# Half of one head's store issued by GpSimd instead of SyncE, in four transfers of 7, 34, 6 and 17 partitions

## The chip, the cores and the metric

The kernel runs on one core of a Trainium2 chip. A core has five engines with an instruction queue each: PE (TensorE, matrix multiplication), DVE (VectorE), ACT (ScalarE), POOL (GpSimd) and SP (SyncE, which computes nothing and issues transfers). Transfers between main memory (HBM) and the on-chip memory (SBUF) are carried by the core's 16 DMA engines. The metric is the device time of one execution in microseconds (us); smaller is better.

## The reference

Linear attention with the feature map elu(x) + 1, for one batch, 32 heads, a sequence of 2048 and a head width of 128, in bfloat16:

```python
phi_q = jnp.where(q > 0, q + 1, jnp.exp(q)) + 1e-6
phi_k = jnp.where(k > 0, k + 1, jnp.exp(k)) + 1e-6
kv = jnp.einsum("bhsd,bhse->bhde", phi_k, v)
z = jnp.einsum("bhsd->bhd", phi_k)
num = jnp.einsum("bhqd,bhde->bhqe", phi_q, kv)
den = jnp.einsum("bhqd,bhd->bhq", phi_q, z)[..., None] + 1e-6
return num / den
```

For each head three arrays of 512 KB are read and one of 512 KB is written: 48 MB in and 16 MB out in all.

## The kernel before

One head is one tile: the 2048 rows of a head lie on 128 partitions, 16 rows (NT) of 128 numbers on each, so a partition holds 4096 contiguous bytes of an input or of the output. The 32 heads run one after the other, and the stages of neighbouring heads overlap.

The steps of a head h, by the names that the program gives them:

- ldk, ldq, ldv: the loads, issued by SP (L367), each into one of 7 buffers.
- ek, em: exp of k on ACT (L384), min with 1 plus 1e-6 on DVE (L387). rkp: max of k with 0 on POOL (L394). Since elu(x) + 1 is min(exp x, 1) + max(x, 0), phi_k is the sum of the two, and it is never formed: PE multiplies each of them by v and adds up in PSUM.
- v1: POOL copies v beside a column of ones (L398), so that kv and z come out of one product. kv: 32 products on PE (L405). kvs: the result goes to SBUF as bfloat16 (L410, DVE).
- T, eq, emq, rqa, rqb: q is transposed on PE (L417) and mapped in the same way on ACT and DVE (L421, L423, L427, L430).
- n: the products with kv and z on PE (L441, L446, L448), into PSUM. r: the reciprocal of the denominator (L464, with L461 ahead of it for the part i = 1). f: DVE multiplies and writes the head's output tile in SBUF (L468). This runs in two parts, f{h}.0 for 12 of the 16 rows of a partition and f{h}.1 for the last 4; the last head has three parts.
- st: SP issues the store (L477), from one of 12 output buffers, as soon as the f steps that it reads are done.

The order on each engine is written out by hand in ORDER (L105 to L166); an engine runs its list from front to back, and each entry waits for semaphores only where its inputs or its buffer need it. Semaphores are counted per engine, and per buffer for transfers. At the end of POOL's list stand v130.0, rkp31.0 and v131.0 (L152). At the end of SP's list, after the last load (ldq31.0), stand the stores st18.0 to st30.0 and the three parts of head 31's (L163, L164).

Three heads are stored in more than one transfer. FEW (L64) gives for heads 4, 8 and 17 a list of (first partition, end partition, n), one transfer each; st_rows and st_parts (L67, L71) read it, and some (L347) issues it. With n = 16 it is an ordinary transfer of those partitions. With another n the program builds the transfer itself, with n as the outermost dimension of both sides (L356), for SP's queue. A partition range of 96 to 128 with n = 4 is a transfer of four times 8 partitions.

After all work SP waits for the semaphore of each output buffer, the last head's last (L492 to L494), and the program ends.

Of the kernel before, what the change touches and what calls it, by code (L numbers as in the profile page):

```python
# [11 lines left out]
NI, NO, NE, NR, NV, NQ, NK = 7, 12, 2, 2, 2, 2, 2  # L12
# [41 lines left out]
def na(h):  # L54
    return NA[h]


def groups(h):
    if h == NH - 1:
        return ((0, 2, 3, 0), (6, 2, 3, 2), (12, 2, 2, 4))  # L60
    return ((0, 4, 3, 0), (12, 2, 2, 4))


FEW = {4: ((0, 96, 16), (96, 120, 3), (120, 128, 4)), 8: ((0, 96, 16), (96, 128, 4)), 17: ((0, 96, 16), (96, 128, 4))}  # L64


def st_rows(h, i):  # L67
    return FEW[h][i] if h in FEW else (0, P, 16)


def st_parts(h):  # L71
    if h in FEW:
        return WHOLE * len(FEW[h])
    return ((0, 6), (6, 12), (12, 16)) if h == NH - 1 else WHOLE
# [22 lines left out]
def rqb_parts(h):  # L97
    if na(h) == 16:
        return ()
    if h == NH - 1:  # L100
# [48 lines left out]
        v16.0 rkp7.0 v17.0 rkp8.0 v18.0 rkp9.0 v19.0 rkp10.0 v110.0 rkp11.0 v111.0 rkp12.0 v112.0 rkp13.0 v113.0  # L149
        rkp14.0 v114.0 rkp15.0 v115.0 rkp16.0 v116.0 rkp17.0 v117.0 rkp18.0 v118.0 rkp19.0 v119.0 rkp20.0 v120.0  # L150
        rkp21.0 v121.0 rkp22.0 v122.0 rkp23.0 v123.0 rkp24.0 v124.0 rkp25.0 v125.0 rkp26.0 v126.0 v127.0 rkp27.0
        rkp28.0 v128.0 v129.0 rkp29.0 rkp30.0 v130.0 rkp31.0 v131.0  # L152
    """,
    "SP": """
        ldk0.0 ldk1.0 ldq0.0 ldv1.0 ldk2.0 ldq1.0 ldv2.0 ldk3.0 ldq2.0 ldv3.0 ldk4.0 ldq3.0 ldv4.0 ldq4.0 ldk5.0
# [22 lines left out]
class Program:  # L178
# [10 lines left out]
    def add(self, eng, key, fn, deps=(), dma=None, inc=True):  # L189
        assert key not in self.op, key  # L190
        self.op[key] = (eng, fn, tuple(deps), dma, inc)
# [71 lines left out]
def bass_standalone__linear_attn_elu__prompt_kernel(nc: bass.Bass, q: bass.AP, k: bass.AP, v: bass.AP, out: bass.AP):  # L263
# [11 lines left out]
    with ExitStack() as es:  # L275
# [25 lines left out]
        pr = Program(sem)  # L301
        add = pr.add
# [44 lines left out]
        def some(e, of, to, p0, p1, n):  # L347
            of = of.rearrange("p j d -> p (j d)")[p0:p1]
            to = to.rearrange("(p j) d -> p (j d)", j=NT)[p0:p1]
            if n == 16:  # L350
                return e.dma_start(to, of)
            to = to.rearrange("(n p) e -> n p e", n=n)
            side = lambda ap, dims: mybir.PhysicalAccessPattern(
                ap=[list(d) for d in dims], offset=ap.offset, dtype=ap.tensor.dtype, memref=ap.tensor.name,
                memsetref=ap.tensor.name + "_set", bass_ap=ap)
            return e.add_instruction(mybir.InstDMACopy(  # L356
                name=nc.get_next_instruction_name(), engine=e.engine,
                ins=[side(of, [of.ap[0], [NT * D, 1], of.ap[1]])], outs=[side(to, to.ap)],
                queue="qSPDynamicHW", mode="Copy"))
# [15 lines left out]
        def head(h):  # L375
# [49 lines left out]
            n = na(h)  # L425
# [47 lines left out]
                                [[m, nb], [1, m], [0, D]]), op=ALU.mult)  # L473
                add("DVE", f"f{h}.{i}", g, [f"r{h}.{i}"] + freed(NO, h, ("st", st_parts)))
            for i, (a, b) in enumerate(st_parts(h)):
                add("SP", f"st{h}.{i}", lambda e, a=a, b=b, i=i: some(
                    e, o_sb[:, h % NO], of[h], *st_rows(h, i)) if h in FEW else e.dma_start(rows(of, h)[:, a:b], o_sb[:, h % NO, a:b]),  # L477
                    [f"f{h}.{j}" for j, (t0, nb, m, b0) in enumerate(groups(h)) if t0 < b and a < t0 + nb * m],
                    dma=f"o{h % NO}")

        for h in range(NH):
            head(h)
# [7 lines left out]
        for e, engine in (("POOL", nc.gpsimd), ("SP", nc.sync), ("ACT", nc.scalar), ("PE", nc.tensor), ("DVE", nc.vector)):  # L490
            pr.emit(e, engine)
        last = f"o{(NH - 1) % NO}"  # L492
        for name in [f"o{s}" for s in range(NO) if f"o{s}" in pr.count and f"o{s}" != last] + [last]:
            nc.sync.wait_ge(pr.get(name), pr.count[name])  # L494


# [26 lines left out]
```

## Time and profile before

| what | value |
|---|---|
| time, median of 3 runs | 168.81 us (168.54 to 169.3) |
| the profiled execution, its own time | 168.74 us |
| its span, first to last instruction | 167.4 us |
| granted TensorE clock, mean | 0.997 |
| HBM read, written | 50.33 MB, 16.78 MB |
| mean DMA rate | 403 GB/s |
| packets on SP's queue (q1), ACT's (q10) | 9663, 144 |
| a store of 512 KB, issue to landing | 19.1 us median, 3.3 to 20.6 |
| last load (ldq31) issued | 129.79 us |
| last copy of GpSimd (v131.0) | 148.68 to 150.17 us |

The profile is taken from one execution; times in it count from the first instruction. The busy time of PE is modelled and doesn't mean that it runs at its peak. The span leaves out 1.34 us of the execution's own time. Six waits of SP at L494 stand at the very end of the span, the first at 166.1 and the last at 167.4.

There is no queue of GpSimd's in the trace: it issues no transfer in this kernel. Besides SP's and ACT's queues there are two that fetch instructions (q8 and q14, 27 packets).

### The profile page before, as it was taken

What the parts mean: (1) busy time and instruction counts of PE and PEld (TensorE: products, weight loads), DVE (VectorE), ACT (ScalarE), POOL (GpSimd) and SP (SyncE); (2) the same over time, 40 slices, a digit from 0 to 9 for tenths busy, and PEclk for the clock granted to TensorE, in tenths of its full rate; (3) what the DMA queues carried; (4) which work ended last, traced back from release to release, by engine and by line L of the source; (5) the groups of instructions that cost most, each with busy time, mean ns of one, the idle gap of its engine ahead of it and who ended that gap; (6) DMA issues with size and microseconds to landing.
All of it is one profiled execution on the core that took longest, in us unless ns stands there. A gap on an engine that the chain in (4) does not pass through costs nothing.

```text
span 167.4 us, 6190 instructions
## 1 busy us (share of the span) xinstructions
PE 156.7 (94%) x2716; PEld 151.2 (90%) x2716; DVE 154.4 (92%) x300; ACT 149.5 (89%) x102; POOL 94.1 (56%) x71
## 2 busy tenths in 40 slices
PE   6999969999999999999999999999999999999740
PEld 2579859999999999999999999999999999999640
DVE  0389999999999999999999999999999999999990
ACT  4899949999999999999999999999999999995700
POOL 2779646656656666655555566666555555670000
PEclk9999999999999999999999999999999999999998
DMA  5999999999999999999999999999999999999995
GB/s 206 432 423 419 395 423 388 419 409 415 411 419 407 407 427 411 417 395 421 415 389 425 418 414 420 426 407 423 402 442 390 425 416 428 405 409 415 414 376 226
DMA packets 9834, 67.51 MB, mean 403 GB/s; under 512 B 2095, under 2 KB 2479, under 8 KB 6831
## 3 DMA queue, kind: packets, MB, share of 16 engines
q1 hardware_dynamic: 9663, 66.59, 97.3%
q8 instruction: 21, 0.34, 0.8%
q10 hardware_dynamic: 144, 0.52, 0.8%
q14 instruction: 6, 0.05, 0.1%
HBM read 50.33 MB, written 16.78 MB: 401 GB/s over the span
## 4 chain that ended last, share of the span: by engine, by line
PE 88%; DVE 8%; issue 0%; POOL 0%; POOLq 0%
PE la L405 34%; PE la L446 17%; PE la L417 17%; PE la L448 16%; PE la L339 5%; DVE la L468 4%; DVE la L387 1%; DVE la L423 1%; DVE la L464 1%; DVE la L430 0%; PE la L441 0%; DVE la L461 0%; DVE la L410 0%; POOL la L324 0%; POOL la L323 0%
## 5 line engine op out<-in xcount | busy, mean ns | idle before, releaser
L394 POOL TENSOR_SCALAR la<-la 128x2048 bf16<-128x2048 bf16 (+1 forms) x32 | 60.5, 1892 | 49.9 <-PE la L405 46.6
L468 DVE TENSOR_TENSOR la<-la 128x1536 bf16<-128x1536 f32 (+2 forms) x65 | 77.7, 1196 | 0.2
L446 PE MATMUL la<-la 128*128 128x129 bf16 x512 | 67.0, 219 | 0.1
L448 PE MATMUL la<-la 128*128 128x129 bf16 x512 | 67.0, 219 | 0.0
L421 ACT ACTIVATE la<-la 128x2048 bf16<-128x2048 bf16 (+2 forms) x35 | 60.2, 1730 | 5.3 <-PE la L448 4.0
L384 ACT ACTIVATE la<-la 128x2048 bf16<-128x2048 bf16 (+1 forms) x33 | 61.3, 1860 | 2.5 <-DMA la<-in_k_dram 2.5
L405 PE MATMUL la<-la 128*128 128x129 bf16 x1024 | 63.4, 220 | 0.0
L405 PEld LDWEIGHTS la<-la 128*128 128x128 bf16 x1024 | 59.5, 98 | 0.4
L448 PEld LDWEIGHTS la<-la 128*128 128x128 bf16 x512 | 49.5, 97 | 0.0
L446 PEld LDWEIGHTS la<-la 128*128 128x128 bf16 x512 | 47.9, 97 | 0.3 <-DVE la L410 0.3
L398 POOL COPY la<-la 128x1024 int32<-128x1024 int32 (+1 forms) x33 | 34.4, 1042 | 5.4 <-PE la L405 3.4
L417 PE MATMUL la<-la 128*128 128x128 bf16 x512 | 34.0, 219 | 1.6 <-DVE la L430 1.6
L427 ACT ACTIVATE la<-la 128x1024 bf16<-128x1024 bf16 (+1 forms) x32 | 33.5, 1047 | 0.0
L417 PEld LDWEIGHTS la<-la 128*128 128x128 bf16 x512 | 30.0, 98 | 2.4 <-DVE la L430 1.8
L387 DVE TENSOR_SCALAR la<-la 128x2048 bf16<-128x2048 bf16 (+1 forms) x33 | 24.8, 751 | 6.1 <-ACT la L384 6.1
L423 DVE TENSOR_SCALAR la<-la 128x2048 bf16<-128x2048 bf16 (+2 forms) x35 | 25.1, 717 | 0.3 <-ACT la L421 0.3
L441 PE MATMUL la<-la 128*128 128x3 bf16 (+1 forms) x128 | 21.6, 169 | 1.8 <-DVE la L468 1.4
L430 DVE TENSOR_SCALAR la<-la 128x1024 bf16<-128x1024 bf16 x31 | 20.5, 661 | 0.0
L441 PEld LDWEIGHTS la<-la 128*128 128x128 bf16 x128 | 12.5, 97 | 2.1 <-DVE la L468 1.5
L464 DVE RECIPROCAL la<-la 128x12 f32<-128x12 f32 (+2 forms) x65 | 12.9, 200 | 1.3 <-PE la L448 0.3
L339 PE MATMUL la<-la 128*128 128x480 bf16 x28 | 8.8, 464 | 1.5 <-POOL la L324 1.5
L410 DVE CAST la<-la 128x129 bf16<-128x129 f32 x32 | 7.8, 244 | 0.1
(16 smaller groups left out, 11.9 us busy)
## 6 DMA issues: line engine op xcount, KB each, us to landing
la<-in_k_dram SPq DMA_DIRECT2D x32, 512.0 KB, 19.2
la<-in_q_dram SPq DMA_DIRECT2D x32, 512.0 KB, 19.6
la<-in_v_dram SPq DMA_DIRECT2D x31, 512.0 KB, 19.4
out_dram<-la SPq DMA_DIRECT2D x28, 512.0 KB, 19.2
out_dram<-la SPq DMA_DIRECT2D x3, 384.0 KB
la<-in_v_dram ACTq DMA_DIRECT2D x1, 512.0 KB, 4.3
out_dram<-la SPq DMA_DIRECT2D x3, 128.0 KB, 3.8
out_dram<-la SPq DMA_DIRECT2D x2, 192.0 KB, 3.4
```

Source lines behind the costliest of these rows:

```text
L384: add("ACT", f"ek{h}.{i}", lambda e, a=a, b=b: e.activation(em_sb[:, h % NE, a:b], k_sb[:, h % NI, a:b], ACT.Exp), over("ldk", h, ld_parts ...
L394: add("POOL", f"rkp{h}.{i}", lambda e, a=a, b=b: e.tensor_scalar(rk_sb[:, h % NR, a:b], k_sb[:, h % NI, a:b], BIG, 0.0, op0=ALU.min, op1=A ...
L398: add("POOL", f"v1{h}.{i}", lambda e, a=a, b=b: e.tensor_copy(v1_sb[:, h % NV, a:b, 0:D].bitcast(i32), v_sb[:, h % NI, a:b].bitcast(i32)), ...
L405: ins = e.matmul(kv_ps, lhsT=src[:, j], rhs=v1_sb[:, h % NV, j, 0:NC], start=(j + part == 0), stop=(j == NT - 1 and part == 1))
L417: ins = e.transpose(xT[:, j], q_sb[:, h % NI, j], ident[:])
L421: add("ACT", f"eq{h}.{i}", lambda e, a=a, b=b: e.activation(emq_sb[:, h % NQ, a:b], xT[:, a:b], ACT.Exp), over("T", h, t_parts, a, b) + fr ...
L423: add("DVE", f"emq{h}.{i}", lambda e, a=a, b=b: e.tensor_scalar(emq_sb[:, h % NQ, a:b], emq_sb[:, h % NQ, a:b], 1.0, EPS, op0=ALU.min, op1 ...
L427: add("ACT", f"rqa{h}", lambda e: e.activation(rq_sb[:, h % NQ, 0:n], xT[:, 0:n], ACT.Relu), over("T", h, t_parts, 0, n) + freed(NQ, h, (" ...
L441: e.matmul(_ap(o_ps[:, :], o + D, [[NC, m]]), lhsT=ones[:], rhs=epsr[:, 0:m], start=True, stop=False, skip_group_check=True)
L446: e.matmul(to, lhsT=emq_sb[:, h % NQ, t], rhs=kvs_sb[:, h % NK, 0:NC], start=late and c == 0, stop=False, skip_group_check=True)
L448: ins = e.matmul(to, lhsT=rq_sb[:, h % NQ, t], rhs=kvs_sb[:, h % NK, 0:NC], start=False, stop=True, skip_group_check=True)
L468: return e.tensor_tensor(out=_ap(o_sb[:, :, :, :], first(o_sb[:, h % NO, t0, 0:1]) - first(o_sb[:, :, :, :]), [[m * D, nb], [D, m], [1, D] ...
```

## The change

FEW gets an entry for head 26 (the 27th): partitions 0 to 64 as an ordinary transfer, and four more ranges, 64 to 71, 71 to 105, 105 to 111 and 111 to 128 (7, 34, 6 and 17 partitions) with n = 0. A part with n = 0 is issued by POOL instead of SP, as an ordinary transfer, and has a semaphore of its own (ob26.1 to ob26.4). The four stand at the end of POOL's list, behind v131.0. The first part keeps its place in SP's list. SP's waits at the end cover every semaphore that begins with "o", the four new ones first. Nothing else on PE, DVE, ACT or POOL moves, and no byte more or less is stored.

```diff
+       26: ((0, 64, 16), (64, 71, 0), (71, 105, 0), (105, 111, 0), (111, 128, 0))}
...
-        rkp28.0 v128.0 v129.0 rkp29.0 rkp30.0 v130.0 rkp31.0 v131.0
+        rkp28.0 v128.0 v129.0 rkp29.0 rkp30.0 v130.0 rkp31.0 v131.0 st26.1 st26.2 st26.3
+        st26.4
...
-            if n == 16:
+            if n in (0, 16):
                 return e.dma_start(to, of)
...
-                add("SP", f"st{h}.{i}", lambda e, a=a, b=b, i=i: some(
+                add("POOL" if h in FEW and not st_rows(h, i)[2] else "SP", f"st{h}.{i}", lambda e, a=a, b=b, i=i: some(
                     e, o_sb[:, h % NO], of[h], *st_rows(h, i)) if h in FEW else e.dma_start(rows(of, h)[:, a:b], o_sb[:, h % NO, a:b]),
                     [f"f{h}.{j}" for j, (t0, nb, m, b0) in enumerate(groups(h)) if t0 < b and a < t0 + nb * m],
-                    dma=f"o{h % NO}")
+                    dma=f"o{h % NO}" if h not in FEW or st_rows(h, i)[2] else f"ob{h}.{i}")
...
-        for name in [f"o{s}" for s in range(NO) if f"o{s}" in pr.count and f"o{s}" != last] + [last]:
+        for name in [name for name in pr.count if name[0] == "o" and name != last] + [last]:
             nc.sync.wait_ge(pr.get(name), pr.count[name])
```

## The prediction

> **What bounds the kernel now.** I read the page first, then the chain of waits, then the end of the run in windows of a quarter to half a microsecond.
>
> ```profile
> span 167.4 us, 6190 instructions
> ...
> PE 156.7 (94%) x2716; PEld 151.2 (90%) x2716; DVE 154.4 (92%) x300; ACT 149.5 (89%) x102; POOL 94.1 (56%) x71
> ...
> DMA  5999999999999999999999999999999999999995
> ...
> q1 hardware_dynamic: 9663, 66.59, 97.3%
> ```
>
> TensorE and the DMA engines are both full from the second slice to the last but two. 97.3% of the DMA time belongs to one queue, SP's. The chain of waits runs over PE, then over VectorE, and stops at the last copy out of PSUM (L468, f31.1 and f31.2):
>
> ```profile
> 161.80 0.02 issue
> 161.82 0.25 DVE la L464 x2
> 162.07 1.53 DVE la L468 x2
> ```
>
> That copy ends at 163.60; the span ends at 167.4. The chain doesn't explain these 3.8 us, so the windows have to:
>
> ```profile
> 159.00:160.00 1.00, 0.41 (x9) 0.42 (x10) 0.93 (x4) 0.00 (x0) 0.00 (x0) 1.00 0.90 369
> 160.00:161.00 1.00, 1.00 (x22) 1.00 (x20) 0.97 (x3) 0.00 (x0) 0.00 (x0) 1.00 0.83 336
> ```
>
> ```profile
> 164.50:164.75 0.25, 0.00 (x0) 0.00 (x0) 0.00 (x0) 0.00 (x0) 0.00 (x0) 1.00 1.01 379
> 164.75:165.00 0.25, 0.00 (x0) 0.00 (x0) 0.00 (x0) 0.00 (x0) 0.00 (x0) 1.00 0.78 295
> ...
> 166.00:166.25 0.25, 0.00 (x0) 0.00 (x0) 0.00 (x0) 0.00 (x0) 0.00 (x0) 1.00 0.58 205
> 166.25:166.50 0.25, 0.00 (x0) 0.00 (x0) 0.00 (x0) 0.00 (x0) 0.00 (x0) 1.00 0.26 90
> 166.50:166.75 0.25, 0.00 (x0) 0.00 (x0) 0.00 (x0) 0.00 (x0) 0.00 (x0) 0.61 0.07 25
> 166.75:167.00 0.25, 0.00 (x0) 0.00 (x0) 0.00 (x0) 0.00 (x0) 0.00 (x0) 0.50 0.06 20
> ```
>
> The last two numbers of a line are the busy share of the 16 DMA engines and GB/s. From 160 to 161 the share is 0.83: about 3 of 16 engines have nothing to do, while the others are full. After 164.75 they fall out one after another; from 166.5 to 167.0 the share is 0.06 to 0.07, that is one engine alone. So the end is the drain of the stores on the most loaded DMA engine, not VectorE and not the latency of the last store.
>
> The trace also keeps a mark for each DMA engine's landing of its part of a store. I sorted the marks of each late store. Head 28's came at 158.28, 158.50, 158.72, then 161.43, 161.44, 161.68, 162.34, and nine from 162.78 to 163.09; head 29's at 159.66, 159.73, 159.96, then 162.67 to 164.41. So three engines are 2.7 to 4.8 us ahead of the rest. Three early marks stand apart in every store from about 109 us on, by 1.2 us then (109.40, next 110.56). The last packet of the last engine ends at 167.00, of the next one at 166.44, and the final wait is released at 167.39.
>
> Which engines are the three? Head 17's store (L64) has a second part dealt to four engines only, 8 rows of 4096 bytes each. A row takes 0.155 us there (8 packets back to back in 1.24 us). The three early marks of its first part are 143.45, 143.66 and 143.88; had these engines carried the second part too, marks at 144.7 to 145.1 would follow. None stands before 146.26. So the three early engines are not among the four that SP's few-way transfers use.
>
> **The change, part by part.** *Removed:* 64 of 128 rows of head 26's store leave SP's queue. Each of 16 engines there moves 4 rows instead of 8: 4 x 0.155 = 0.62 us less on each. SP issues a shorter transfer between two others that wait for VectorE anyway; that is nothing on the path.
>
> *Added:* GpSimd issues four transfers, of 7, 34, 6 and 17 rows, after its last copy (v131.0, L398), which ends at 150.17. Their source, f26.1, ends at 143.72, so nothing has to be waited for, and nothing is queued behind them on GpSimd. The other loads have all been issued by then (ldq31 at 129.8), so no load shares an engine with them for long.
>
> How 7, 34, 6 and 17 rows are dealt to engines no row of this trace shows for GpSimd. The nearest rows are SP's: 128 and 96 rows leave sixteen marks, a transfer with an outer dimension of 4 leaves four marks, one of 3 leaves three. Equal parts, as many as the outer dimension allows, would put one row each on 7 engines, 17 rows each on 2 (34 in two halves), one row each on 6, and 17 rows on 1. If each transfer goes on where the one before stopped, that is 16 engines once around: thirteen with 1 row and three with 17. Against the 4 rows that each had, thirteen engines lose 3 rows, 3 x 0.155 = 0.47 us, and three gain 13 rows, 2.02 us.
>
> The bounds are these. Best: the three loaded engines are the three early ones. They land head 29's store at 159.7 and head 30's, which is issued behind f30.1 (ends 160.53), at 163.08; of these 3.4 us only 8 x 0.155 = 1.24 are transfer, so about 2.2 us are idle, and 2.02 us more fit. The end then moves with the thirteen others: -0.47 us. Worst: a loaded engine is a late one that never idles. The next-to-last engine goes from 166.44 to 168.46, +1.46 us on the end; the very last from 167.00 to 169.02, +2.02 us. In the middle, an even deal: 0. I take the best case, since the gap is three engines wide, the deal by SP's rows gives three loaded engines, and the idle 2.2 us hold the 2.02; but which three they are stays open, and both ends go into the range.
>
> GpSimd's cost of issuing is not in the trace either. SP's issue of a full store is 1.06 us (median of L477); that times four is 4.2 us, so 150.2 to 154.4, all behind GpSimd's last work. At the lower bound it costs nothing. At the upper bound it starves: the last copy itself shows a stretch,
>
> ```profile
> 144.06 1.04 POOL L398 COPY la<-la 128x1024 int32<-128x1024 int32 x1
> ...
> 148.68 1.49 POOL L398 COPY la<-la 128x1024 int32<-128x1024 int32 x1
> ```
>
> 0.45 us longer where VectorE's L423 (148.59 to 149.28) ran beside it. Even 0.45 us twice per transfer gives 4 x 1.96 = 7.8 us, done by 158.0, before the early engines run dry. VectorE's own L423 took 0.69 beside that copy and 0.63 at 153.13 without it, so the reverse cost is about 0.06 us per instruction, and VectorE may slip: late engines have backlog until 166. The Trainium skill (SBUF — State Buffer, "SBUF: two separate sides") says that a VectorE operation in a two-port mode locks GpSimd out while it writes descriptors, and tells of a transfer of 620 ns that took 3100. The stretched copy agrees in kind; by that figure four transfers would be an estimated 12.4 us and end near 162.6.
>
> *Four more waits* of SP at L494 come ahead of the others; the waits there show 28 ns each and pass while the last stores are draining: 0.
>
> **Sum.** Profiled execution: span 167.4 - 0.47 = 166.93, and its own time 168.74 - 0.47 = 168.27 (the 1.34 us around the span stay). That execution lies 0.07 under the median of the runs, 168.81, so the time I predict is 168.81 - 0.47 = 168.34, -0.28%. What a measurement can tell from no change is about 0.5%, 0.84 us: the forecast is inside it.
>
> **Rivals.**
>
> *1. The rows are dealt evenly, or the change of queue is all that happens.* Then the bytes per engine are as before and the time is 168.8. If rows go in blocks, at most the rows over 16 rounded up on each engine from the lowest on, the lowest six get 1+3+1+2 = 7 rows for 4: +0.47 us at worst, 169.3; at best the last engine is one of the top four, -0.47 us. For it: no row shows GpSimd's deal. Against it: SP's rows do show few-way deals. The Trainium skill (DMA: Bandwidth & Descriptors, "Rules for kernel authors") speaks against the change here: spreading transfers over SP, ACT and GpSimd doesn't help, because they run on the same 16 engines, which by itself would give 168.8. The share of 0.83 from 160 to 161 shows that the 16 are not equally loaded, so a deal that differs can help. Its section "Why a DMA increments its semaphore by 16 and not by 1" has both deals for GpSimd, the divisor with a cursor that goes round, and the blocks for some copies; no run here shows either.
>
> *2. The loaded engines are late ones (the other side).* One mechanism: 17 rows where there were 4, on an engine without idle time. It decides from the point where a loaded engine's own end plus 2.02 us, less its idle time after 150, comes after 167.00: an engine that ends at 166.44 would need 1.46 us of idle time, and the late ones have none. By the above: 168.81 + 1.46 = 170.3, or 170.8 on the very last. For it: nine of sixteen marks of head 28 are in the late group, so a blind choice of three would nearly always hit one. Against it: only the width and depth of the gap.
>
> *3. GpSimd issues late.* If each transfer takes d, the last of them, 17 rows on one engine, is issued at 150.2 + 4d. To its first byte it needs about 1.3 us (f29.1 ends at 157.13, its store's first landing is at 159.66, and 1.24 of that is transfer), then 17 x 0.155 = 2.64, and 0.39 to the release. The span then ends no earlier than 154.5 + 4d: later than the forecast's 166.93 from d = 3.1 us on. At 3.5 us it is 168.5 (a time of 169.9), at 4 us 170.5 (171.9). For it: VectorE is 75 to 100% busy in each microsecond from 150 to 160. Against it: the stretch that the trace shows is 0.45 us.
>
> **Chances.** Forecast 0.56, rival 1 0.15, rival 2 0.18, rival 3 0.11. Faster by over 0.5% needs 0.84 us, more than the thirteen engines lose; it happens only if the lone last engine (0.56 us behind the others) also disappears, which can be since the runs of before differ by 0.76 us: 0.16, out of the forecast. Slower by over 0.5%: rival 2 and most of rival 3, 0.27. Within: the other 0.57. The range goes from 167.7 (the forecast less 0.6, the last engine gone) to 170.3 (rival 2's first price). The forecast's own range is 167.7 to 168.8.
>
> **What would show it.** A new queue with four transfers, 64 rows of 4096 bytes, from 150 to about 155, issued behind v131.0. In the windows the share from 160 to 161 goes from 0.83 towards 1.0 (the three now have work), and the fall after 164.75 begins no earlier but ends near 166.5 instead of 167.0. Head 26's store on SP's queue is a 256 KB transfer. Wrong is the forecast if the share from 160 to 161 stays at 0.83 or falls and one to three engines run alone beyond 167 (rival 2), if the queue's packets come after 160 (rival 3), or if the tail looks as before (rival 1).

## The result and the profile after

| what | before | after |
|---|---|---|
| median of 6 runs, us | 168.80 (168.54 to 169.30) | 169.85 (169.21 to 170.05) |
| the profiled execution, its own time | 168.74 | 169.9 |
| its span | 167.4 | 168.5 |
| last copy out of PSUM ends | 163.60 | 161.81 |
| last packet of the last DMA engine ends | 167.00 | 168.10 |

The kernel became slower: the ratio is 1.0056, with a 95% interval of 1.0034 to 1.0078. The forecast was a gain of 0.47 us, to 168.34; measured is a loss of 1.05. The time still lies inside the range on record, 167.7 to 170.3. From here on line numbers above 64 are larger than those of before (L468 is L470, L398 is L400, L347 is L349).

The page of after, its totals and its two store queues:

```profile
span 168.5 us, 6196 instructions
...
PE 156.8 (93%) x2716; PEld 151.2 (90%) x2716; DVE 152.1 (90%) x300; ACT 149.5 (89%) x102; POOL 96.6 (57%) x75
...
DMA  5999999999999999999999999999999999999994
...
q1 hardware_dynamic: 9599, 66.33, 96.4%
...
q0 software_dynamic: 176, 0.26, 0.4%
```

64 packets have gone from q1 (9663 before) to a queue of GpSimd's, q0, which has 0.4% of the DMA time: the change does what it says. The last step of the chain of waits in after:

```profile
160.28 1.53 DVE la L470 x2
```

The computation is done at 161.81, 1.8 us sooner than in before's profile, and the end still comes 1.1 us later. So the end isn't VectorE's, and the windows at the end are the place to read (busy time of PE, PEld, DVE, ACT, POOL, then PE clock, DMA share, GB/s):

```profile
160.00:161.00 1.00, 0.00 (x0) 0.00 (x0) 0.97 (x3) 0.00 (x0) 0.00 (x0) 1.00 1.01 393
164.50:164.75 0.25, 0.00 (x0) 0.00 (x0) 0.00 (x0) 0.00 (x0) 0.00 (x0) 0.50 0.87 348
164.75:165.00 0.25, 0.00 (x0) 0.00 (x0) 0.00 (x0) 0.00 (x0) 0.00 (x0) 0.50 0.64 252
...
166.50:166.75 0.25, 0.00 (x0) 0.00 (x0) 0.00 (x0) 0.00 (x0) 0.00 (x0) 0.50 0.35 125
166.75:167.00 0.25, 0.00 (x0) 0.00 (x0) 0.00 (x0) 0.00 (x0) 0.00 (x0) 0.50 0.21 72
167.00:167.50 0.50, 0.00 (x0) 0.00 (x0) 0.00 (x0) 0.00 (x0) 0.00 (x0) 0.50 0.08 31
167.50:168.00 0.50, 0.00 (x0) 0.00 (x0) 0.00 (x0) 0.00 (x0) 0.00 (x0) 0.50 0.07 25
```

The engines fall out later: from 166.5 to 166.75 five or six of 16 still work (0.35; one in before, 0.07), and one works alone until 168.1. The share from 160 to 161 went from 0.83 to 1.01, which the prediction had named as a sign of its own deal. GpSimd's part, by its timeline and by the group of its issues (nanoseconds, shortest, median and longest):

```profile
147.22 1.15 POOL L400 COPY la<-la 128x1024 int32<-128x1024 int32 x1 [0.29 <-DMA la<-in_v_dram]
148.32 2.53 POOL L353 DMA_DIRECT2D out_dram<-la  x4
```

```profile
L353 POOL DMA_DIRECT2D out_dram<-la x4: 505/594/856, 148.3 to 150.3; - x4
```

The four transfers are issued in 2.53 us, by 150.85, and the first packet of their rows starts at 152.61. Each leaves sixteen landing marks: 153.25 to 154.69, 154.26 to 157.52, 154.59 to 157.71 and 155.42 to 158.30.

One view of the trace carries the rest of this document, its records of single packets. A store packet of 4096 bytes takes 159 ns as a rule. I count those that take over 200 ns after 145 us and call them long packets. Before has 7, in pairs behind instruction fetches (the first of one pair starts before 145); after has 29, 18 of them from 155.5 to 161, and the longest takes 832 ns. Their excess over 159 ns sums up to 1.3 us in before and 5.7 us in after, over all 16 engines. The records don't name the engine of a packet. On a busy engine a packet starts 3 to 4 ns before the end of the one ahead of it, and by that a single engine's packets can in places be followed.

### The profile page after: what moved, and what is told of

Its sections match the earlier page's. It is cut to its first block, busy times and chain, and to the rows that moved or that the text cites. A ratio compares the mean times of both kernels' runs of the same rounds, so it can differ in the third digit from the quotient of the medians.

```text
span 168.5 us, 6196 instructions
## 1 busy us (share of the span) xinstructions
PE 156.8 (93%) x2716; PEld 151.2 (90%) x2716; DVE 152.1 (90%) x300; ACT 149.5 (89%) x102; POOL 96.6 (57%) x75
## 4 chain that ended last, share of the span: by engine, by line
PE 91%; DVE 4%; issue 0%; POOL 0%; POOLq 0%
PE la L407 34%; PE la L448 18%; PE la L419 17%; PE la L450 16%; PE la L341 5%; DVE la L470 3%; DVE la L466 0%; PE la L443 0%; DVE la L425 0%; DVE la L463 0%; POOL la L326 0%; POOL la L325 0%; DVE la L412 0%; POOLq L326 0%; POOLq L510 0%
## 5 line engine op out<-in xcount | busy, mean ns | idle before, releaser
L470 DVE TENSOR_TENSOR la<-la 128x1536 bf16<-128x1536 f32 (+2 forms) x65 | 77.6, 1195 | 0.2
L400 POOL COPY la<-la 128x1024 int32<-128x1024 int32 (+1 forms) x33 | 34.2, 1035 | 4.8 <-PE la L407 3.4
L389 DVE TENSOR_SCALAR la<-la 128x2048 bf16<-128x2048 bf16 (+1 forms) x33 | 23.1, 699 | 6.1 <-ACT la L386 6.1
L425 DVE TENSOR_SCALAR la<-la 128x2048 bf16<-128x2048 bf16 (+2 forms) x35 | 24.5, 700 | 0.5 <-ACT la L423 0.5
```

Source lines behind the costliest of these rows:

```text
L400: add("POOL", f"v1{h}.{i}", lambda e, a=a, b=b: e.tensor_copy(v1_sb[:, h % NV, a:b, 0:D].bitcast(i32), v_sb[:, h % NI, a:b].bitcast(i32)), ...
L425: add("DVE", f"emq{h}.{i}", lambda e, a=a, b=b: e.tensor_scalar(emq_sb[:, h % NQ, a:b], emq_sb[:, h % NQ, a:b], 1.0, EPS, op0=ALU.min, op1 ...
L470: return e.tensor_tensor(out=_ap(o_sb[:, :, :, :], first(o_sb[:, h % NO, t0, 0:1]) - first(o_sb[:, :, :, :]), [[m * D, nb], [D, m], [1, D] ...
```

## The experiments

Kernels that send a part of the store to GpSimd hold the change's routing (n = 0 goes to POOL, with a semaphore of its own) and differ in FEW and in the lists of ORDER; the diffs show what differs from before, cut to the lines that matter. A third number of 16 or 0 in FEW says SP or GpSimd. Ratios are against runs of before on the same chip. A ratio isn't the quotient of the two medians, and the two can differ by some tenths of a microsecond. Long packets are counted in one profiled execution of each kernel.

### What about it costs: GpSimd, the deal, or the cut?

One transfer of GpSimd's for the whole half, which is dealt evenly:

```diff
+       26: ((0, 64, 16), (64, 128, 0))}
...
+        rkp28.0 v128.0 v129.0 rkp29.0 rkp30.0 v130.0 rkp31.0 v131.0 st26.1
```

> Head 26's other half (64 rows) is one GpSimd transfer of 64 partitions, 4 rows to each of 16 engines under any deal. Theory Q (GpSimd's queue itself makes the DMA engines slower, by long packets while and after it has work): 169.2 to 170.0, close to the 169.85 of the change, and packets well over 200 ns between 150 and 161. Theory D (only the deal of the rows costs): 168.8, no more long packets than in the kernel before.

Measured: 169.65 us, ratio 1.0049 [1.0028, 1.0071], 34 long packets. Without the uneven deal nearly all of the loss is there, so the deal alone isn't the cause.

61 rows and 3, to see GpSimd's deal:

```diff
+       26: ((0, 64, 16), (64, 125, 0), (125, 128, 0))}
```

> GpSimd issues 61 and 3 partitions. If rows are dealt by the largest divisor up to 16, 61 rows fall on one engine: 57 rows more, 57 x 0.155 = 8.8 us; less at most 2.2 us of idle time on an early engine, the time is 175 to 178. If they are dealt in blocks of 4 on 15 engines and one more, no engine gets more than 1 row too many: 168.8 to 170, as in the run with one even transfer.

Measured: 169.16, 1.0029 [1.0014, 1.0045], 25 long packets. The marks of the 61 rows stand at 153.98 to 155.31, those of the 3 rows at 154.45 to 155.93. On one engine 61 rows would have taken 61 x 0.155 = 9.5 us; the issue begins at 148.32, 7.0 us before the last of the 61 rows' marks. A prime number of rows doesn't go to one engine.

The second half issued by ACT ("POOL" in the change's routing line becomes "ACT"):

```diff
-        eq30.0 rqa30 eq31.0 eq31.1 eq31.2 rqa31
+        eq30.0 rqa30 st26.1 eq31.0 eq31.1 eq31.2 rqa31
```

> The same 64 rows, one even transfer issued by ACT between rqa30 and eq31.0 instead of by GpSimd. A second queue as such costing time (theory Q in its wide form): 169.2 to 170.0. Only GpSimd's queue costing: 168.8, within 0.3 of the kernel before; ACT's issue (about 1 us) lies where ACT has slack before eq31.

Measured: 170.34, 1.0077 [1.0051, 1.0102], 25 long packets. The loss doesn't need GpSimd. This form holds ACT's work for head 31 up as well (the last copy ends at 162.48), so its size says little.

Both halves by SP, in two transfers, 0 to 64 and 64 to 128:

```diff
+       26: ((0, 64, 16), (64, 128, 16))}
...
-        st24.0 st25.0 st26.0 st27.0 st28.0 st29.0 st30.0 st31.0 st31.1 st31.2
+        st24.0 st25.0 st26.0 st26.1 st27.0 st28.0 st29.0 st30.0 st31.0 st31.1 st31.2
```

> Head 26's store on SP in two transfers of 64 partitions, next to each other. No theory expects anything: 168.8 within 0.3. If the time is higher, splitting the store is itself a cost.

Measured: 169.83, 1.0059 [1.0042, 1.0075], 27 long packets. No theory that I had gave this a cost, and it has all of it: same queue, same bytes, 4 rows for each engine twice instead of 8 once. This run turned the case. What was left to ask is whether the moment at which the stores run matters, and what about a half.

### Is it the moment?

After's profile shows the computation 1.8 us early. That begins near 20 us, where DVE's em of head 3 and POOL's rkp of head 4 meet or don't. The timelines of DVE and POOL in before, and then in after:

```profile
19.90 2.37 DVE L387 TENSOR_SCALAR la<-la 128x2048 bf16<-128x2048 bf16 x1
...
19.74 1.99 POOL L394 TENSOR_SCALAR la<-la 128x2048 bf16<-128x2048 bf16 x1 [0.31 <-PE la L405]
```

```profile
19.81 0.68 DVE L389 TENSOR_SCALAR la<-la 128x2048 bf16<-128x2048 bf16 x1
...
20.00 2.25 POOL L396 TENSOR_SCALAR la<-la 128x2048 bf16<-128x2048 bf16 x1 [0.65 <-PE la L407]
```

Where POOL starts first, DVE's instruction takes 2.37 us instead of 0.68. The rival theory was that early stores are what costs. Before once more, unchanged, to see which way it falls:

> The kernel before, profiled once more, against itself. In its first profile VectorE's L387 at 19.90 took 2.37 us beside a GpSimd operation, against 0.68 in the changed kernel, and all later work of the engines came 1.8 us later; the end came 1.1 us earlier all the same, and from 151 to 161 hardly any store packet took over 200 ns. Theory P (the phase of the engines' work sets the packets): time 168.7; if this profile shows the late phase, few long packets again; if the early one, a time near 169.7 and many long packets. Theory S (head 26's store in two pieces is what costs): 168.7 and few long packets in either phase.

Measured: 168.77, 0.9996 [0.9985, 1.0007], 6 long packets; its last copy ended at 161.81, as in after. And before with rkp4 held behind em3, which fixes the early order:

```diff
-    return []
+    return ["em3.0"] if (name, h) == ("rkp", 4) else []
```

> The kernel before, whole store on SP, with GpSimd's rkp4 made to wait for VectorE's em3.0, so that VectorE isn't held up at 20 us and the engines' work comes about 1.8 us earlier, as in the changed kernel. Theory P: 169.5 to 170, with long packets from 151 to 161. Theory S: 168.7, few long packets. A third way (engines earlier, so the stores drain earlier): 167 to 168.4.

Measured: 168.76, 0.9993 [0.9979, 1.0006], 6 long packets, last copy at 161.74. The early order costs nothing and brings nothing. The change with the order reversed (this diff is against the change's kernel):

```diff
-                    ... op0=ALU.min, op1=ALU.add), [f"ek{h}.{i}"])
+                    ... op0=ALU.min, op1=ALU.add), [f"ek{h}.{i}"] + (["rkp4.0"] if h == 3 else []))
```

> The changed kernel with VectorE's em3.0 made to wait for GpSimd's rkp4, so that the engines' work comes about 2 us later, as in the kernel before. Theory P: 168.3 to 169.0, few long packets. Theory S: 169.5 to 170, long packets as in the changed kernel.

Measured: 169.43, 1.0034 [1.0022, 1.0046], 28 long packets, last copy at 163.83, which is the moment of before's first profile. The loss is there too, 0.49 us against 1.05; the intervals of the two ratios overlap, so whether the moment has a part in its size is open. The same edit on the two halves of SP:

> The store of head 26 in two halves on SP, with VectorE's em3.0 made to wait for GpSimd's rkp4 (engines' work about 2 us later). Theory P: 168.5 to 169.0. Theory S: 169.5 to 170, as with the two halves without the wait (169.83).

Measured: 169.91, 1.0056 [1.0038, 1.0073], 20 long packets. Here the edit overshot: the last copy ended at 166.59, so a part of the time is computation, and this run decides little. The theory that the moment alone makes the loss falls by the two before it. The early run of before also takes a sign of the prediction away, its windows:

```profile
160.00:161.00 1.00, 0.00 (x0) 0.00 (x0) 0.97 (x3) 0.00 (x0) 0.00 (x0) 1.00 1.02 414
...
160.00:162.00 2.00, 0.00 (x0) 0.00 (x0) 1.78 (x4) 0.00 (x0) 0.00 (x0) 1.00 0.97 393
...
167.00:168.00 1.00, 0.00 (x0) 0.00 (x0) 0.00 (x0) 0.00 (x0) 0.00 (x0) 0.50 0.00 0
```

The share of 1.02 stands there without the change. It tells when the stores were issued, not how their rows were dealt.

### What about a half?

Two halves along the row, each of 128 partitions and 2048 bytes, by SP, and then with the second one routed to GpSimd, again with a semaphore of its own:

```diff
-    return ((0, 6), (6, 12), (12, 16)) if h == NH - 1 else WHOLE
+    return ((0, 6), (6, 12), (12, 16)) if h == NH - 1 else HALVES if h == 26 else WHOLE
```

> Head 26's store on SP in two transfers again, but cut along the row: all 128 partitions, 2048 bytes of each. Theory G (the geometry of 64 partitions, 4 rows for each engine, makes the long packets): 168.8 to 169.0 (packets of 2048 bytes cost some 0.05 us more per engine), few packets far over their usual length. Theory C (cutting the store in two as such): 169.6 to 170.

> The same cut along the row, the second half issued by GpSimd behind v131.0, from all 128 partitions. Theory G, where GpSimd's queue costs nothing by itself: 168.7 to 169.0. Theory Q (GpSimd's queue costs): 169.4 or more. Theory C: 169.6 or more.

Measured: 168.84, 1.0001 [0.9992, 1.0011], and 168.91, 0.9997 [0.9984, 1.0009]; 6 long packets in each. Two transfers cost nothing, and half of the store on GpSimd's queue costs nothing.

Three ranges by SP, of which the middle one takes 32 partitions from either half:

```diff
+ 26: ((0, 32, 16), (32, 96, 16), (96, 128, 16))}
```

> Head 26's store on SP in partitions 0 to 32, 32 to 96 and 96 to 128, so that the middle transfer has 4 rows for each engine as in the halves, but spans both halves of the partitions. If long packets come from sixteen engines reading one half of the partitions at a time, the middle one has none, only the outer ones, with half the rows: 169.2 to 169.4. If they come from where 4 rows per engine fall in HBM, the middle one has them too: 169.7 or more.

Measured: 168.87, 1.0003 [0.9991, 1.0015], 7 long packets. 64 partitions in one transfer are free if they are 32 to 96. The outer ranges of 32, which I had thought might cost something, are free too.

Quarters, which keep each half together for 4 rows in a row (2 and 2), and one half whole with the other cut:

```diff
+ 26: ((0, 32, 16), (32, 64, 16), (64, 96, 16), (96, 128, 16))}
```

> Head 26's store on SP in four transfers of 32 partitions, 2 rows for each engine, every one within one half of the partitions. If reading one half of the partitions at a time is what makes long packets: 169.4 or more. If it takes 4 rows at a time per engine for it: 168.8, few long packets.

```diff
+ 26: ((0, 64, 16), (64, 96, 16), (96, 128, 16))}
```

> Head 26's store on SP in partitions 0 to 64, 64 to 96 and 96 to 128: one 64-partition transfer instead of two. If each half costs for itself: about half of the two halves' 1.1 us, 169.3, with long packets; if the first half is the whole cost, 169.8; if it takes both, 168.8.

Measured: 169.49, 1.0040 [1.0022, 1.0058], 26 long packets; and 169.20, 1.0032 [1.0014, 1.0049], 21. So it isn't the size of a transfer: 32 partitions cost here and were free above. What the costly forms share and the free ones lack is that all 16 engines, if rows are dealt evenly, take 4 rows in a row from one half of the partitions. A run with the same quarters in alternating order, which would test this wording, is not among the experiments.

Is it the reading from SBUF or the writing to HBM? One kernel reads 0 to 64 and writes the rows of 32 to 96; the other reads 32 to 96 and writes the rows of 0 to 64 (the fourth number is the first row written, which `some` takes as one more argument):

```diff
+ 26: ((0, 64, 16, 32), (64, 96, 16, 0), (96, 128, 16, 96))}
```

> Head 26's store on SP with partitions 0 to 64, 64 to 96 and 96 to 128 read, but written to rows 32 to 96, 0 to 32 and 96 to 128 of the head, so that head 26's output is permuted. What is read is as in the costly run (64, 32, 32), what is written as in the free one (32, 64 in the middle, 32). If the long packets come from the reading side: 169.2 and some 15 more long packets than the 6 of the kernel before. If from the writing side: 168.8 and no more than 6 or 7.

```diff
+ 26: ((32, 96, 16, 0), (0, 32, 16, 64), (96, 128, 16, 96))}
```

> The reverse: partitions 32 to 96, 0 to 32 and 96 to 128 are read and written to rows 0 to 64, 64 to 96 and 96 to 128, head 26's output permuted. Reading side: 168.8 and 6 or 7 long packets. Writing side: 169.2 and some 15 more long packets.

Measured: 169.75, 1.0059 [1.0041, 1.0078], 22 long packets, for reading a half; 168.87, 1.0007 [0.9984, 1.0031], 8 long packets, for writing one. The reading side is what costs. The price was expected at 169.2, as in the run with the same three reads (169.20), and came out half a microsecond above it; why is open. The windows of the first, then of the second:

```profile
160.00:162.00 2.00, 0.00 (x0) 0.00 (x0) 1.79 (x5) 0.00 (x0) 0.00 (x0) 1.00 0.91 345
...
167.00:168.00 1.00, 0.00 (x0) 0.00 (x0) 0.00 (x0) 0.00 (x0) 0.00 (x0) 0.50 0.17 64
```

```profile
160.00:162.00 2.00, 1.67 (x32) 1.49 (x28) 1.93 (x6) 0.00 (x0) 0.00 (x0) 1.00 0.89 363
...
167.00:168.00 1.00, 0.00 (x0) 0.00 (x0) 0.00 (x0) 0.00 (x0) 0.00 (x0) 0.50 0.00 0
```

With a busier share (0.91 against 0.89) the first moves less (345 GB/s against 363): its engines are occupied by packets that take longer. (The second's profile fell in the late order, the first's in the early one; before in its early run has a share of 0.97 and 393 GB/s.) And the first has work left after 167 (0.17 of the engines), where the second has none. The same is seen with SP's two halves, and beside it with 32 to 96, in the windows of these two:

```profile
160.00:162.00 2.00, 0.00 (x0) 0.00 (x0) 1.53 (x2) 0.00 (x0) 0.00 (x0) 1.00 0.96 375
...
167.00:168.00 1.00, 0.00 (x0) 0.00 (x0) 0.00 (x0) 0.00 (x0) 0.00 (x0) 0.50 0.11 41
```

```profile
160.00:162.00 2.00, 0.00 (x0) 0.00 (x0) 1.79 (x5) 0.00 (x0) 0.00 (x0) 1.00 0.96 391
...
167.00:168.00 1.00, 0.00 (x0) 0.00 (x0) 0.00 (x0) 0.00 (x0) 0.00 (x0) 0.50 0.01 5
```

The same share of 0.96 moves 375 and 391 GB/s. The Trainium skill (SBUF — State Buffer, "Door 1: The DMA port swizzle (why `[64,N]` ≈ `[32,N]`)") says that partitions 0 to 63 reach only 8 of 16 ports of the SBUF and 64 to 127 the other 8. The runs agree as far as 64 partitions go: 32 to 96 takes 8 from either side by that rule and is free, at 168.87. The two outer ranges of 32 lie on one side too, and they were free in the same run, which the rule doesn't tell. The ports themselves are in no trace.

### What is left of the deal

The change with its 64 rows taken from 32 to 96, where reading costs nothing, first in transfers of 7, 34, 6 and 17, and then in one:

```diff
+ 26: ((0, 32, 16), (32, 39, 0), (39, 73, 0), (73, 79, 0), (79, 96, 0), (96, 128, 16))}
```

> The change with GpSimd's four transfers of 7, 34, 6 and 17 kept, but laid over partitions 32 to 96; SP stores 0 to 32 and 96 to 128. No 64-partition transfer is left on SP. If that transfer was the cost and the deal is in blocks on the lowest engines: between 168.3 and 169.3 by which engines end last, 168.8 if the late ones get 4 rows as before. If the deal put 17 rows on three early engines as the prediction had it: 168.3. If GpSimd's four transfers are themselves what costs: 169.4 to 170.

```diff
+ 26: ((0, 32, 16), (32, 96, 0), (96, 128, 16))}
```

> GpSimd stores partitions 32 to 96 of head 26 in one transfer, 4 rows for each engine; SP stores 0 to 32 and 96 to 128. It differs from e13 (169.44) in the deal alone: one transfer instead of 7, 34, 6 and 17 partitions. If e13's cost is its uneven deal: 168.8 and 6 or 7 long packets. If GpSimd's queue beside a cut by partitions costs: 169.3 or more.

Measured: 169.44, 1.0034 [1.0022, 1.0045], 13 long packets; and 168.87, 0.9994 [0.9983, 1.0005], 8. The two differ only in how GpSimd's 64 rows are cut into transfers. The windows of the four, then of the one:

```profile
166.00:167.00 1.00, 0.00 (x0) 0.00 (x0) 0.00 (x0) 0.00 (x0) 0.00 (x0) 0.50 0.40 145
167.00:168.00 1.00, 0.00 (x0) 0.00 (x0) 0.00 (x0) 0.00 (x0) 0.00 (x0) 0.50 0.06 22
```

```profile
166.00:167.00 1.00, 0.00 (x0) 0.00 (x0) 0.00 (x0) 0.00 (x0) 0.00 (x0) 0.50 0.30 107
167.00:168.00 1.00, 0.00 (x0) 0.00 (x0) 0.00 (x0) 0.00 (x0) 0.00 (x0) 0.50 0.02 6
```

With four, the last packets of the five latest engines end at 167.71, 167.23, 167.09, 167.01 and 166.81; with SP alone on the same three ranges the four latest end at 167.26, 166.68, 166.66 and 166.56. So some late engines end 0.4 to 0.6 us later, about three rows. By the medians it is 169.44 - 168.86 (before beside it) = 0.58 us.

In the trace of the four transfers, GpSimd's packets on one engine can be followed without a gap, one packet of SP's between any two of them: a row at 152.85 and a mark, rows at 153.32, 153.63 and 153.94 and a mark, a row at 154.41 and a mark, rows at 154.88 and 155.19 and a mark at 155.50. That is 1 + 3 + 1 + 2 = 7 rows on one engine, from all four transfers, as rival 1's blocks have it for the lowest six. In the prediction's deal no engine has rows of more than one of the four.

Not all of the 0.58 us need be those rows. Three of the four ranges lie in one half of the partitions, two of them (73 to 79 and 79 to 96) next to each other, and this trace has 13 long packets with 2.6 us of excess against 8 with 1.4. How much of the loss that makes isn't shown.

### A version that beats both

Since a late engine sets the end, a few-way transfer made smaller can take rows off late engines. Head 17's second part goes from 32 rows on four engines to 16, and the rest of it is dealt to all:

```diff
-17: ((0, 96, 16), (96, 128, 4))
+17: ((0, 112, 16), (112, 128, 4))
```

> The kernel before with head 17's store dealt as 112 partitions to all and 16 to the first four engines, instead of 96 and 32: the four lose 3 rows (0.47 us), the others gain 1 (0.16). If the engine that ends last (167.00, with an instruction fetch of 0.31 us at 164) is one of the four: 168.3 to 168.6. If it is another: 168.9 to 169.1. Theory G's geometry isn't in it, unless 7 rows per engine make long packets as well.

Measured: 168.52 (168.24 to 168.79), 0.9983 [0.9973, 0.9993], against 168.77 for before beside it; 6 long packets. It is faster than both kernels, by 0.25 us over before. The last engine ends at 166.89 and five others from 166.69 to 166.84; in the early run of before it is 167.03, with the next at 166.64: the ends have come closer together. By the two cases that were set out, the engine that ends last is one of the four.

## Why the prediction was wrong, point by point

**The end is the drain of the stores on the most loaded engine: right.** The last copy came 1.8 us earlier and the end 1.1 us later, and before's time is the same with its computation held to the early order (0.9993).

**Removed, 64 rows, "4 x 0.155 = 0.62 us less on each": this step failed, and it is most of the miss.** It took away 4 x 0.155 us and left the other 64 rows of SP at 0.155 each, whichever partitions they come from. The forecast never priced the cut at partition 64. What remained on SP is a store that reads 0 to 64 alone, and GpSimd's rows read 64 to 128 alone. SP's two halves without GpSimd and without the odd deal cost 169.83 - 168.73 = 1.10 us; 32 to 96 in their place costs 0.10, within what is measured as none. In place of 4 x 0.155 less on each engine stand packets of 205 to 832 ns on some of them, 5.7 us of excess in all against 1.3 in before. The engine that ends last in after can be followed back from 168.10 without idle time to one of these, 428 ns at 160.69; that the others pass theirs on in the same way is argued.

**Added, thirteen engines with 1 row and three with 17: failed as well.** The 61 rows showed that a number of rows that 16 doesn't divide isn't put on one engine, and the followed engine has 7 rows where the forecast had 1 or 17. The rows over 16 rounded up, from the lowest engine on (rival 1's blocks: 7 on the lowest six), fit: 3 rows more are 0.47 us on late engines at worst, and 0.58 was measured with no half on SP. The Trainium skill (DMA: Bandwidth & Descriptors, "Why a DMA increments its semaphore by 16 and not by 1") has that deal, as an exception, for some copies of GpSimd's; these two runs agree with it: 61 rows spread, 7 rows on one engine. Which of the 16 the followed engine is isn't in the trace.

**The two don't add up.** One alone costs 1.10, the other alone 0.58, and the change 169.85 - 168.80 = 1.05. In after the last engine, the one with the 428 ns packet, ends 0.93 us behind the next; rows that go to other engines don't show behind it, and GpSimd's even half is only 0.2 us faster than the four transfers. That last figure is less than the spread of either (168.93 to 170.28, 169.21 to 170.05), so how the two share the loss in after is open. Nor is the size of the cut's part settled: kernels that read a half with all engines lost between 0.34 us (0 to 64, 64 to 96, 96 to 128 on SP) and 1.10 (SP's two halves), and the same kernel scatters (168.58 to 170.14 for the two halves, 168.69 to 169.13 for the halves along the row).

**Three early engines that idle: right, and beside the point.** In the early run of before three engines end at 163.37, 163.41 and 163.50, the next at 165.12. But nothing chose them.

**GpSimd's issue lies behind its last work: right, and over-priced.** 2.53 us against 4.2 to 7.8; rival 3 needed 3.1 us for each transfer (its sum counts the 0.39 us from the last packet to the mark twice, so 3.2), and the longest took 0.856. **The queue and the waits are free:** with GpSimd storing half of each row, or 32 to 96 in one transfer, the time is before's.

**Rival 2** came near with its price (170.3), and one engine does work alone beyond 167, but not by its mechanism: that is luck. **Rival 1** named the right deal with nearly the right price, 0.47 at worst. Its best case is mis-summed: the top four engines get no row by these blocks, and lose 4 x 0.155 = 0.62 and not 0.47. And its case that an even deal costs nothing fails where the cut is at 64 (0.92 us, 169.65 against 168.73).

**Open:** why 2 rows of a half in a row, as the outer ranges of 32 have them, are absorbed and 4 are not; what sets the size of the loss; which engines the early ones are, and why.

## What to carry to other kernels

When DMA engines run full to the end, a transfer's price is not rows times a packet's time: ask which partitions it reads, and take them from both halves (32 to 96, or all 128 with shorter rows) when a store has to be split. Put one and the same share on every engine, since the end belongs to the latest of them, or move rows off the latest on purpose and look at the sixteen ends to see whether it helped. And undo a change's parts one at a time with the plainest form first: SP with the same cut, without the engine that the change was about, is what settled this one.

## What the runs showed of the hardware that I had not expected

- A store that reads one half of the partitions with 4 rows in a row for each of 16 engines comes with single packets of up to 621 ns in place of 159 and costs 0.3 to 1.1 us at the end (SP's own transfers, medians against before; with GpSimd's transfers beside them packets took up to 1108 ns, in the change with the order reversed); reading 32 to 96, or writing rows of one half, costs nothing.
- GpSimd issued transfers of 6 to 34 rows in 0.505 to 0.856 us each, with VectorE busy all the time from 148 to 151, and each left sixteen landing marks, those with 6 and 7 rows too. So the marks don't tell which engines got rows.
- One VectorE instruction took 2.37 us in before where a GpSimd instruction had started 0.16 us ahead of it, and 0.68 in after where it started first. In the second profile of before VectorE's also started first (18.96 against 19.91); the computation ends 1.8 us sooner there (161.81 against 163.60), and the last packet at the same time (167.03 against 167.00).
